# Chunk attention and Fourier mixing on one core: one add moved to VectorE, one weight conversion moved back on ScalarE

## Chip, cores and metric

The kernel runs on one core of a Trainium2 chip. The metric is the device time of one execution in microseconds (us); the time of a kernel is the median of its runs.

## What is computed

q, k, v and the output are float32, the two weights float64. With B = 8 batches, H = 8 heads, S = 576 tokens and D = 64:

```python
# attention in chunks of 64 tokens, each chunk on its own
scores = (q_c @ k_c.T) / sqrt(D)
attn = softmax(scores)
x = (attn @ v_c)                      # bridged to (B, S, 512)
# Fourier mixing and a two-layer network
mixed = real(fft(fft(x, axis=1), axis=2))
u = x + mixed
un = (u - mean(u)) / sqrt(var(u) + 1e-6)
out = u + relu(un @ w_ch1) @ w_ch2    # 512 -> 2048 -> 512
```

## The kernel before

**Tiles.** A tile is 128 tokens by 512 columns. Each batch has two lower tiles (LO, the first four chunks), two upper tiles (HI, the last four, kept mirrored, with a 513th column), and a middle chunk; the middle chunks of two batches share one tile (RE, "rest"). `at[HI, 1, 0]` is the first upper tile of batch 1, the second batch. The upper half of a Fourier transform of real data mirrors the lower half, so `mixed(i)` makes one product `mix` in PSUM for lower tile i and upper tile i together. `both` turns it into `y` on VectorE with two instructions (L850 and L851), and `added` (L857) adds `y` to the rows of each tile in `xall`: the lower and the middle tiles on VectorE, the upper tiles on GpSimd. `means` takes mean and variance of both tiles (VectorE, L705 and L706) and then 1/sqrt(var + eps) of both at once (ScalarE, L709 and L710).

**Groups.** The network runs on groups of four tiles: group g for g = 0 to 7 is batch g, and a ninth group holds the four rest tiles. `normed(g, s)` makes the normalised rows `un` of tile s (for group 1, and for tiles 0 and 1 of group 0, three ScalarE instructions, L996 to L998; otherwise VectorE, L1000). `turned` transposes `un` on TensorE (L399) and copies it out of PSUM to `unT` (L1013). Attention and Fourier mixing of batch b + 1 are woven by hand into the network of group b, step by step. The order on each engine is that in which the program issues the instructions.

**Group 0.** Its network has plain products: w_ch1 at L1219 (with the first weight rows at L944) and w_ch2 at L1260. From group 1 on seven products of halves take the place of eight (L1309 and L1363; the last two groups do the second layer in L1427), with sums and differences of weight blocks that are made once, on GpSimd, while group 0 is still in the network: `keep2` for w_ch2 (L1095) and `keep1` for w_ch1 (L1078). SyncE stores these sums (L1107, L1082, L1114).

**Weight conversion.** The weights arrive as 32 pieces of 128 by 512 float64 values, which the kernel turns into float32 from their bits, as `round_weight(i)` does in a pipeline: the head of piece i and the tail of piece i - 1. The head masks the exponent (VectorE, L372) and the high fraction bits (VectorE, L382), and has three ScalarE instructions: `fraction` (L364, needs L382), `exponent` (L367, needs L372) and `power_` (L370, needs `exponent`). The tail adds the low fraction bits to the fraction (VectorE, L379, needs L364), adds the sign to the power (VectorE, L380, needs L370), and multiplies the two (VectorE, L388). It then frees the piece's landing space and issues the next load (SyncE, L348). A head can be given a list `later`; its three ScalarE instructions are then not issued but put into the list, in the order fraction, exponent, power_. Piece 1 does so in `fourier_early`, with the list `put_off`:

```python
round_weight(1, put_off, "h")     # head only
...
idle[0] = mid
for do in put_off[:2]:            # fraction, exponent
    do()
keep_warm(3)
```

The third, `power_`, follows after the first two pairs of normalised tiles, as `put_off[2]()`. `keep_warm` issues matmuls of no use.

Of the kernel before, what the change touches and what calls it, by code (L numbers as in the profile page):

```python
# [11 lines left out]
ALU = mybir.AluOpType  # L12
# [4 lines left out]
def kernel(  # L17
# [32 lines left out]
    nc = tc.nc  # L50
# [117 lines left out]
    LO, HI, RE = "lo", "hi", "rest"  # L168
# [10 lines left out]
    at = {t: n for n, t in enumerate(tiles)}  # L179
# [17 lines left out]
    def kind(n):  # L197
        return tiles[n][0]
# [140 lines left out]
    def raw(i):  # L339
        return spaces[raws[i]].bitcast(U32).rearrange("p (f r) -> p f r", r=2)  # L340

    def load_weight(i):

        fit = [r for r in free if (i < N_EARLY or r < N_LATE) and (i < N_LAST or r > 1)]
        if i < len(pieces) and fit:
            raws[i] = fit[0]
            free.remove(fit[0])
            nc.sync.dma_start(out=raw(i).rearrange("p f r -> p (f r)"), in_=pieces[i][1].bitcast(U32))  # L348

    def round_weight(i, later=None, parts="ht"):  # L350

        head, tail = "h" in parts and i < len(pieces), "t" in parts and 0 < i <= len(pieces)
        if head:
            w, t = pieces[i][0], raw(i)
            hi, wi = t[:, :, 1], w.bitcast(U32)  # L360
            p = power[i] = three_p.tile([128, 512], U32, tag="o", name="power")

            def fraction(w=w, wi=wi):
                nc.scalar.activation(out=w, in_=wi, func=ACTF.Copy, scale=2.0 ** -20, bias=1.0)  # L364

            def exponent(p=p):
                nc.scalar.activation(out=p, in_=p, func=ACTF.Relu, scale=-1.0, bias=top[:, 0:1])  # L367

            def power_(p=p):
                nc.scalar.activation(out=p, in_=p, func=ACTF.Relu, scale=-8.0, bias=top[:, 1:2])  # L370

            nc.vector.tensor_scalar(p, hi, 0x7FF00000, None, ALU.bitwise_and)  # L372
            if later is None:
                exponent()
                power_()
        if tail:
            w_, t_ = pieces[i - 1][0], raw(i - 1)
            p_ = power.pop(i - 1)
            nc.vector.scalar_tensor_tensor(w_, t_[:, :, 0], 2.0 ** -52, w_, ALU.mult, ALU.add)  # L379
            nc.vector.scalar_tensor_tensor(p_, t_[:, :, 1], 0x80000000, p_, ALU.bitwise_and, ALU.bitwise_or)  # L380
        if head:
            nc.vector.tensor_scalar(wi, hi, 0x000FFFFF, None, ALU.bitwise_and)  # L382
            if later is None:
                fraction()
            else:
                later += [fraction, exponent, power_]
        if tail:
            nc.vector.tensor_tensor(out=w_, in0=w_, in1=p_.bitcast(FP32), op=ALU.mult)  # L388

            r = raws.pop(i - 1)  # L390
            if i - 1 + len(spaces) < N_EARLY or r < N_LATE:
                free.append(r)
            load_weight(max(raws, default=i - 1) + 1)
# [320 lines left out]
    def z_sets(z, pm, i, turn_, first=False):  # L714


        for s in range(2):
            for q_ in range(4):
                k, r = (q_ // 2 + turn_) % 2, q_ % 2
                T, p = 2 * k + s, slice(32 * q_, 32 * q_ + 32)  # L720
                d0_ = T * HQ if i < NM else s * HQ
                nc.tensor.matmul(  # L722
                    out=z[r][k][:, s * NE:(s + 1) * NE], lhsT=pm[i][p, d0_:d0_ + HQ],
                    rhs=tk[p, NM - 1 - i if i < NM else NM, k],
                    start=first and s == 0, stop=False, skip_group_check=True,
                )

    def mid_products(outs, pm, i):
        p, m0 = (slice(0, 128), DM) if i < NM else (slice(CH, 128), 2 * HQ)
        for g, out_ in enumerate(outs):  # L730
            c0, c1 = halves[g % 2]
            nc.tensor.matmul(
                out=out_[:, 0:c1 - c0], lhsT=pm[i][p, m0 + g // 2:m0 + g // 2 + 1], rhs=tk[p, NM - 1 - i if i < NM else NM, 0, c0:c1],
                start=False, stop=i == NM, skip_group_check=True,
            )

    def z_space():


        odd = [ps_t.tile([128, 512], FP32, tag="pt", name="z") for _ in range(2)]  # L740
        even = ps_a.tile([128, 2, 512], FP32, tag="att", name="more_z")
        zs[1:] = even, odd
        return odd, [even[:, k] for k in range(2)]

    def z_odd():
        for k in range(2):
            nc.scalar.copy(zs[0][:, 2 * k:2 * k + 2, 1], zs[2][k][:, 0:2 * NE].rearrange("p (t f) -> p t f", t=2))
# [10 lines left out]
    def z_middle(outs):  # L758
        for g, out_ in enumerate(outs):
            c0, c1 = halves[g % 2]  # L760
            nc.scalar.copy(middle[:, g // 2, c0:c1], out_[:, 0:c1 - c0])
# [33 lines left out]
    def fourier(b):  # L795
        h = b % 2
        zf = one_p.tile([128, 4 * NL + 16], FP32, tag="zf", name="zf")
        zf = zf[:, 0:4 * NL].rearrange("p (t f) -> p t f", t=4)
        zs[0] = one_p.tile([128, 8 * NE], FP32, tag="two", name="zs").rearrange("p (t r f) -> p t r f", t=4, r=2)
        pm = [pms.pop((b, i)) for i in range(NM + 1)]  # L800


        z = z_space()
        for i in range(NM + 1):
            z_sets(z, pm, i, 0, i == 0)
        outs = [z[0][0][32 * g:32 * g + 1, 2 * NE:] for g in range(4)]
        for i in range(NM):
            mid_products(outs, pm, i)
        nc.scalar.copy(middle[:, 0, 0:1], outs[0][:, 0:1])
        yield  # L810
        if b == 1:
            yield True
        mid_products(outs, pm, NM)
        for i in range(NM):
            z_sets(z, pm, i, 1)
        z_middle(outs)
        z_odd()
        if b == 1:
            round_next()
            z_joined()  # L820
        else:
            yield
            z_joined()
        nc.scalar.copy(zs[0][0:1, 2], middle)
        for i in range(NM):
            z_tile(zf, i)
        if h == 0:
            z_rest(h)
        yield

        def mixed(i):
            mix = ps_t.tile([128, 512], FP32, tag="pt", name="mix")
            zt = zr.rearrange("p t h f -> p t (h f)") if i == NM else zf[:, :, 128 * i:128 * (i + 1)]
            for T, (cols, tab) in enumerate((
                (slice(0, HM + 1, 2), ce),
                (slice(1, HM, 2), co),
                (slice(0, DM, 2), cx),
                (slice(HM + 1, DM, 2), so),
            )):
                nc.tensor.matmul(  # L840
                    out=mix[:, cols], lhsT=zt[:, T], rhs=tab,
                    start=(T == 0), stop=(T == 3), skip_group_check=True,
                )
            y = three_p.tile([128, XW], FP32, tag="y", name="y")
            nc.scalar.copy(y[:, 0:HM + 1], mix[:, 0:HM + 1])
            nc.scalar.copy(y[:, DM:DM + 1], mix[:, 0:1])
            return y, mix

        def both(y, mix):
            nc.vector.tensor_tensor(out=y[:, DM - 1:HM:-1], in0=y[:, 1:HM], in1=mix[:, HM + 1:DM], op=ALU.subtract)  # L850
            nc.vector.tensor_tensor(out=y[:, 1:HM], in0=y[:, 1:HM], in1=mix[:, HM + 1:DM], op=ALU.add)  # L851
            return y

        def added(y, n):
            x, w = xt(n), DM + (kind(n) == HI)
            eng = nc.gpsimd if kind(n) == HI else nc.vector
            eng.tensor_tensor(out=x[:, 0:w], in0=y[:, 0:w], in1=x[:, 0:w], op=ALU.add)  # L857

        for i in range(NM + h):
            y = mixed(i)  # L860
            if i == 0 and h == 1:
                z_rest(h)
            y = both(*y)
            ns = [rests[b // 2]] if i == NM else [at[LO, b, i], at[HI, b, i]]
            for n in ns:
                added(y, n)
            means(ns)
            yield

    def fourier_early():  # L870
# [43 lines left out]
        n, m = CH // 2, CH // 4  # L914
# [15 lines left out]
                    start=(T == 0), stop=(T == 2), skip_group_check=True,  # L930
                )
        idle[0] = mid
        for do in put_off[:2]:
            do()
        keep_warm(3)
        yield
        ups = ps_a.tile([128, 2, 512], FP32, tag="att", name="up_a")
# [11 lines left out]
        for i in range(NM):  # L949
# [13 lines left out]
            if i == 0:  # L963
                normed(0, 1)
                turned(0, 0)
                keep_warm(1)
        put_off[2]()
        put_off.clear()
        columns(1)
        normed(0, 2)  # L970
# [490 lines left out]
    with tc.manual_schedule():  # L1461
# [31 lines left out]
        put_off, first_ups = [], []  # L1493

        def round_next(later=None):
            nonlocal n_w
            if n_w <= len(pieces):
                round_weight(n_w, later)
                n_w += 1
# [159 lines left out]
```

## Time and profile before

| | us |
|---|---|
| median of 3 runs | 1060.59 (1060.47 to 1060.66) |
| profiled execution | 1062.15 |
| its span, from the first to the last instruction | 1060.3 |
| TensorE busy | 1043.2 (98%) |
| VectorE busy | 626.4 (59%) |
| GpSimd busy | 431.5 (41%) |
| ScalarE busy | 315.2 (30%) |

The profile is of one execution, and its times count from the start of its span. The granted TensorE clock has a mean of 0.996 of full speed. The busy share is an average over stages that differ: the first 42 us (attention and Fourier mixing of batch 0 before any network can run), the network of group 0 up to about 190 us with all weight conversions beside it, and seven further groups and the rest tiles after it. In the profile PE is TensorE's matmuls, PEld its weight loads, DVE is VectorE, ACT is ScalarE, POOL is GpSimd, SP is SyncE, and L857 is line 857 of the kernel.

### The profile page before, as it was taken

What the parts mean: (1) busy time and instruction counts of PE and PEld (TensorE: products, weight loads), DVE (VectorE), ACT (ScalarE), POOL (GpSimd) and SP (SyncE); (2) the same over time, 40 slices, a digit from 0 to 9 for tenths busy, and PEclk for the clock granted to TensorE, in tenths of its full rate; (3) what the DMA queues carried; (4) which work ended last, traced back from release to release, by engine and by line L of the source; (5) the groups of instructions that cost most, each with busy time, mean ns of one, the idle gap of its engine ahead of it and who ended that gap; (6) DMA issues with size and microseconds to landing.
All of it is one profiled execution on the core that took longest, in us unless ns stands there. A gap on an engine that the chain in (4) does not pass through costs nothing.

```text
span 1060.3 us, 20226 instructions
## 1 busy us (share of the span) xinstructions
PE 1043.2 (98%) x7482; PEld 852.8 (80%) x7482; DVE 626.4 (59%) x1339; ACT 315.2 (30%) x744; POOL 431.5 (41%) x555
## 2 busy tenths in 40 slices
PE   8899998999999999999999999999999999999998
PEld 6655444788888888888888888888888888888887
DVE  3798996874567465664565645735664666543332
ACT  4688573233113311332022312331133102201200
POOL 3401119753425151244134421524252777661272
PEclk8999999999999999999999999999999999999999
DMA  8757666777678447973577358844753759999264
GB/s 163 227 182 221 173 192 227 204 230 240 223 211 236 135 141 222 246 201 110 184 228 225 119 169 233 253 128 154 226 159 100 265 183 352 345 389 321 90 208 149
DMA packets 167088, 219.10 MB, mean 207 GB/s; under 512 B 77228, under 2 KB 111020, under 8 KB 161614
## 3 DMA queue, kind: packets, MB, share of 16 engines
q1 hardware_dynamic: 155978, 211.98, 64.2%
q0 software_dynamic: 9024, 4.91, 2.1%
q8 instruction: 60, 0.98, 0.4%
q10 hardware_dynamic: 1988, 0.92, 0.3%
q14 instruction: 38, 0.31, 0.1%
HBM read 183.61 MB, written 34.08 MB: 205 GB/s over the span
## 4 chain that ended last, share of the span: by engine, by line
PE 86%; DVE 4%; SPq 3%; ACT 3%; DMA 2%; issue 1%; POOL 0%; DVEq 0%; ACTq 0%; POOLq 0%
PE pa L1309 20%; PE pb L1309 15%; PE pb L1363 15%; PE pa L1363 12%; PE dn L1427 8%; PE dn L1260 3%; PE pt L399 3%; PE up L1219 2%; PE z L722 2%; PE xp L501 2%; SPq L265 2%; PE mix L840 2%; DMA xall<-in_moe_w_ch_dram 1%; PE sc L451 1%; PE up_a L1219 0%
## 5 line engine op out<-in xcount | busy, mean ns | idle before, releaser
L1309 PE MATMUL pa<-unT,wa 128*128 128x256 f32 x736 | 175.3, 381 | 0.2 <-DVE xall L1317 0.2
L1309 PEld LDWEIGHTS pa<-unT,wa 128*128 128x128 f32 x736 | 138.1, 190 | 19.6 <-DVE xall L1317 0.6
L1309 PE MATMUL pb<-wa 128*128 128x256 f32 x448 | 106.6, 381 | 0.0
L1309 PEld LDWEIGHTS pb<-wa 128*128 128x128 f32 x448 | 84.3, 190 | 11.5
L1363 PE MATMUL pa<-wb,h 128*128 128x256 f32 x384 | 87.2, 380 | 0.0
L1363 PE MATMUL pb<-wb,h 128*128 128x256 f32 x384 | 86.4, 379 | 0.0
L1193 POOL TENSOR_TENSOR h<-h 128x256 f32<-128x256 f32 x48 | 40.8, 858 | 97.8 <-DVE wb L1191 91.3
L1363 PEld LDWEIGHTS pa<-wb,h 128*128 128x128 f32 x384 | 71.8, 190 | 9.7
L1363 PEld LDWEIGHTS pb<-wb,h 128*128 128x128 f32 x384 | 72.0, 190 | 9.4
L1044 POOL DMA_DIRECT2D out_dram<-wb x28 | 18.8, 674 | 121.1 <-DVE wb L1380 71.9
L1315 DVE TENSOR_TENSOR wa<-pb,wa 128x256 f32<-128x256 f32 x56 | 23.7, 424 | 63.4 <-ACT wa L1314 63.4
L1309 PE MATMUL pb<-unT,wa 128*128 128x256 f32 x256 | 60.6, 379 | 0.1
L1325 ACT ACTIVATE h<-pa 128x256 f32<-128x256 f32 x64 | 24.6, 384 | 115.0 <-PE pa L1309 114.6
L1260 PE MATMUL dn<-wb,h 128*128 128x512 f32 x128 | 57.4, 596 | 0.0
L1314 ACT COPY wa<-pa 128x256 f32<-128x256 f32 x56 | 20.9, 373 | 121.4 <-PE pa L1309 121.4
L1309 PEld LDWEIGHTS pb<-unT,wa 128*128 128x128 f32 x256 | 48.6, 190 | 7.1 <-DVE wa L1315 0.5
L1207 POOL TENSOR_TENSOR h<-h 128x512 f32<-128x512 f32 x34 | 42.6, 1272 | 27.6 <-ACT h L1331 24.1
L1309 PE MATMUL pa<-wa 128*128 128x256 f32 x224 | 53.9, 383 | 0.0
L483 ACT COPY pT<-pt 128x512 f32<-128x512 f32 x36 | 21.0, 583 | 107.2 <-PE pt L399 107.0
L1331 ACT ACTIVATE h<-h 128x512 f32<-128x512 f32 x64 | 39.9, 629 | 39.8 <-DVE h L1330 39.7
L1219 PE MATMUL up<-unT,wa 128*128 128x512 f32 x108 | 49.4, 598 | 0.0
L857 POOL TENSOR_TENSOR xall<-y,xall 128x513 f32<-128x513 f32 x14 | 22.3, 1590 | 61.1 <-DVE y L851 45.0
(312 smaller groups left out, 2138.9 us busy)
## 6 DMA issues: line engine op xcount, KB each, us to landing
wa<-s SPq DMA_DIRECT2D x196, 256.0 KB
wb<-s SPq DMA_DIRECT2D x42, 1024.0 KB
wb<-s SPq DMA_DIRECT2D x32, 512.0 KB
xall<-in_moe_w_ch_dram SPq DMA_DIRECT2D x22, 512.0 KB
q<-in_q_dram SPq DMA_DIRECT2D x96, 112.0 KB
k<-in_k_dram SPq DMA_DIRECT2D x96, 112.0 KB
s<-part SPq DMA_DIRECT2D x32, 256.0 KB
v<-in_v_dram SPq DMA_DIRECT2D x124, 64.0 KB
```

Source lines behind the costliest of these rows:

```text
L399: nc.tensor.transpose(pt[:, j, :], src(j), ident)
L857: eng.tensor_tensor(out=x[:, 0:w], in0=y[:, 0:w], in1=x[:, 0:w], op=ALU.add)
L1193: nc.gpsimd.tensor_tensor(out=h1[:, m, hi], in0=h1[:, m, lo], in1=h1[:, m, hi], op=ALU.subtract)
L1207: eng.tensor_tensor(out=out_, in0=a, in1=b, op=op)
L1219: nc.tensor.matmul(out=up, lhsT=w1[:, kk, m * 128:(m + 1) * 128], rhs=unT[:, kk], start=(kk == 0), stop=(kk == KD - 1), skip_group_check=True,
L1260: nc.tensor.matmul(out=dn, lhsT=h1[:, m, s * 128:(s + 1) * 128], rhs=w2[:, m, :], start=(m == 0), stop=(m == KF - 1),)
L1309: nc.tensor.matmul(out=dst, lhsT=w[:, kk, r], rhs=rhs[o][:, kk], start=(o in (0, 1) and kk == 0), stop=(kk == 1), skip_group_check=True,)
L1315: nc.vector.tensor_tensor(out=b, in0=pbs[r][:, 0], in1=a, op=ALU.add)
L1325: nc.scalar.activation(out=h1[:, m, lo], in_=dst, func=ACTF.Relu)
L1331: nc.scalar.activation(out=h1[:, HF + m], in_=h1[:, HF + m], func=ACTF.Relu)
L1363: nc.tensor.matmul(out=dst, lhsT=lhs[:, m], rhs=w[:, m], start=(o in (0, 2) and m == 0), stop=(m == HF - 1), skip_group_check=True,)
L1427: nc.tensor.matmul(out=dst, lhsT=lhs[:, m], rhs=w[:, m], start=(fresh and not half and m == 0), stop=(m == 3), skip_group_check=True,)
```

## The change

Three edits. In `added`, the upper tile `at[HI, 1, 0]` is added on VectorE; the other upper tiles stay on GpSimd. In `fourier_early`, `exponent` of piece 1 stays at its place, while `fraction` of piece 1 is issued behind `power_`. In `round_weight(2)`, which holds the tail of piece 1, the two tail instructions are issued in the opposite order, so that the one that needs `fraction` comes second.

```diff
@@ round_weight
         if tail:
             w_, t_ = pieces[i - 1][0], raw(i - 1)
             p_ = power.pop(i - 1)
-            nc.vector.scalar_tensor_tensor(w_, t_[:, :, 0], 2.0 ** -52, w_, ALU.mult, ALU.add)
-            nc.vector.scalar_tensor_tensor(p_, t_[:, :, 1], 0x80000000, p_, ALU.bitwise_and, ALU.bitwise_or)
+            for part in (1, 0) if i == 2 else (0, 1):
+                if part == 0:
+                    nc.vector.scalar_tensor_tensor(w_, t_[:, :, 0], 2.0 ** -52, w_, ALU.mult, ALU.add)
+                else:
+                    nc.vector.scalar_tensor_tensor(p_, t_[:, :, 1], 0x80000000, p_, ALU.bitwise_and, ALU.bitwise_or)
@@ added, in fourier
-            eng = nc.gpsimd if kind(n) == HI else nc.vector
+            eng = nc.gpsimd if kind(n) == HI and n != at[HI, 1, 0] else nc.vector
             eng.tensor_tensor(out=x[:, 0:w], in0=y[:, 0:w], in1=x[:, 0:w], op=ALU.add)
@@ fourier_early
         idle[0] = mid
-        for do in put_off[:2]:
-            do()
+        put_off[1]()
         keep_warm(3)
...
         put_off[2]()
+        put_off[0]()
         put_off.clear()
         columns(1)
```

The order of instructions is otherwise unchanged on every engine; the number of instructions is the same. In the changed kernel lines have a number higher by 3 from the first edit on (by 2 between the two edits of `fourier_early`): L857 is L860 there.

## The prediction

> **What bounds the kernel now.** I read the page first, then the table by stage, then what TensorE waited for, then the chain and the timelines at the two places that the diff touches.
>
> ```profile
> PE 1043.2 (98%) x7482; PEld 852.8 (80%) x7482; DVE 626.4 (59%) x1339; ACT 315.2 (30%) x744; POOL 431.5 (41%) x555
> ```
>
> TensorE is busy for 98% of the span, so only what closes one of its few holes can shorten the run. The windows view, with columns for the stretch, PE, PEld, DVE, ACT, POOL busy, clock, DMA share and GB/s, says where they are.
>
> ```profile
> 42.00:54.00 12.00, 10.16 (x66) 8.32 (x66) 10.70 (x25) 10.85 (x38) 0.00 (x0) 1.00 0.57 136
> 160.00:170.00 10.00, 8.42 (x28) 4.17 (x26) 3.62 (x9) 3.22 (x10) 8.72 (x7) 1.00 0.80 249
> 170.00:182.00 12.00, 9.80 (x63) 4.97 (x64) 8.84 (x15) 5.04 (x15) 11.32 (x9) 1.00 0.50 178
> 201.00:1060.00 859.00, 855.01 (x6100) 743.84 (x6099) 466.84 (x1003) 193.14 (x496) 362.35 (x463) 1.00 0.66 209
> ```
>
> The holes lie at 42 to 54 us and at 160 to 182 us. The waits view, asked for TensorE from 205 us on, lists nothing: whatever TensorE gains before 205 us should reach the end unshortened. For 42 to 205 us it lists (total, times, longest):
>
> ```profile
> PE pt L399 <- DVE y L851: 2.6, 2, 2.1
> PE pt L399 <- ACT un L998: 1.6, 2, 1.1
> PE pt L399 <- ACT unT L1013: 1.1, 1, 1.1
> ```
>
> The second line is the hole at 47 us, the other two are at 170 to 182 us. The diff touches both.
>
> **Part 1, the conversion on ScalarE.** The chain of waits around 44 us (start, duration, what):
>
> ```profile
> 44.03 0.10 ACT zr L924
> 44.14 0.52 ACT wa L364
> 44.65 0.61 ACT power L367
> 45.26 0.19 ACT rstd L709
> ```
>
> ScalarE is the path here. `fraction` of weight piece 1 (L364, 0.52) and `exponent` (L367, 0.61) stand ahead of the first rstd; the VectorE result that this rstd needs is complete at 44.40 (L706, 44.22 + 0.18). Taking L364 away starts the rstd 0.52 earlier. The later rstds are not caught by VectorE: their L706 end at 45.98, 47.51 and 49.09, and ScalarE would come to them at 46.33, 48.48 and 49.38. So un moves from 46.13 to 45.61 and TensorE's transposes from 47.00 and 48.68 to 46.48 and 48.16; its idle time there (1.05 and 0.54) covers 0.52.
>
> L364 comes back behind the third late instruction, `power_` (L370), which moves from 50.34 to 49.82. L364 then runs from about 50.45 (0.63 behind L370, as at 53.42 and 54.05) to 51.06. Behind it stands the copy of unT for the third transposes. It starts at 51.69 after 0.64 of idle ScalarE, so at 51.17 after the change: L364 fits with 0.1 to spare, and is costed at nothing. Without that cover, the copy would be late by the overhang, at worst 0.52, and Part 1 would give nothing.
>
> The VectorE instruction that needs L364 is L379 of piece 1. The swap of the two tail instructions puts L380 first, which needs only L370. L380 would run at 50.75 to 51.36, L379 start at 51.36, 0.3 after L364 ends; L388 finishes the piece at 52.97 instead of 53.49. TensorE needs the piece at 53.70 instead of 54.22, so the margin stays 0.73. **Part 1: -0.52.** From there to 160 us the weight pieces' conversions, the attention of the second batch and the loads are released by one another, so they should move together; VectorE's waits for a load (0.67, 1.21 and 0.22 at 140, 144 and 149 us) are on loads issued after its own earlier steps.
>
> **Part 2, the add on VectorE.** The timeline of all engines (start, duration, engine, line, what, idle before and who ended it):
>
> ```profile
> 160.62 0.86 DVE L857 TENSOR_TENSOR xall<-y,xall 128x512 f32<-128x512 f32 x1
> ...
> 160.89 1.71 POOL L1095 TENSOR_TENSOR xall<-wb,xall 128x512 f32<-128x512 f32 x1
> ...
> 161.51 0.69 DVE L705 BATCH_NORM_STATS2 bst<-xall 128x6 f32<-128x512 f32 x1
> ...
> 162.57 1.25 POOL L1095 TENSOR_TENSOR yall<-wb 128x512 f32<-128x512 f32 x1
> ...
> 163.79 1.27 POOL L857 TENSOR_TENSOR xall<-y,xall 128x513 f32<-128x513 f32 x1
> ...
> 165.09 0.69 DVE L705 BATCH_NORM_STATS2 bst<-xall 128x6 f32<-128x512 f32 x1 [2.67 <-POOL xall L857]
> ...
> 166.04 0.30 ACT L709 ACTIVATE rstd<-st,eps 128x2 f32<-128x2 f32 x1 [7.53 <-DVE st L706]
> ```
>
> The upper tile's add stands in GpSimd's queue behind two L1095 (sums of w_ch2) that still have to run when its y is complete, and ends at 165.06; VectorE waits 2.67 for it, then ScalarE's rstd, two normalised row tiles, the copy of the next mix at 169.06, L850, L851 at 169.96, and TensorE's transposes at 170.53, which need the PSUM buffer that L851 frees. All of that is one chain behind the rstd.
>
> After the change the add follows L857 of the lower tile on VectorE, with no wait of its own, and can start at 161.39 (independent neighbours overlap by 0.08). Its price is bounded below by the fastest row of L857 on VectorE, 0.69. It is likely more, since GpSimd is inside an add then. Rows where both engines add from SBUF:
>
> ```profile
> 174.77 1.26 POOL L1078 TENSOR_TENSOR wa<-wa 128x512 f32<-128x512 f32 x1
> 175.01 1.57 DVE L857 TENSOR_TENSOR xall<-y,xall 128x512 f32<-128x512 f32 x1
> ...
> 184.23 1.33 POOL L1095 TENSOR_TENSOR yall<-wb,yall 128x512 f32<-128x512 f32 x1
> ...
> 184.36 1.49 DVE L1033 TENSOR_TENSOR unT<-unT 128x256 f32<-128x256 f32 x1
> ```
>
> At 175.01 VectorE's add ends 0.55 after GpSimd's (176.58 against 176.03): it was held until GpSimd was through. At 184.36 L1033 follows another VectorE add directly, with GpSimd's add waiting since 184.23; GpSimd goes first (ends 185.56) and L1033, alone 0.41, ends at 185.84. The engines alternate. L1095 at 160.89 takes 1.71 because it waited for the lower tile's add; so it goes next, to 162.60, and the upper tile's add ends at 162.60 + 0.55 = 163.15, a price of 1.76. The upper bound is that the four L1095 still to come also go first: 1.23 each (their steps from 165.02 on), 4.92 more. I take 1.76, from the rows nearest in time and operands.
>
> From the add's end to the rstd: L705 (-0.08 + 0.69), L706 (0.04 + 0.18), L705 (-0.09 + 0.69), L706 (0.04 + 0.18), and 0.04 to ScalarE, 1.69 in all. The rstd starts at 164.84 instead of 166.04. TensorE's transposes come at 169.33; it is through with its own work at 168.42, so it still idles 0.9 and gains all of 1.20. The next links (the second upper add, still on GpSimd, which is free by 168.0, before the 169.36 at which that add is now released; its L705; the mix of the middle chunk; TensorE at 175.12 and 181.69) hang on this one and keep their distances. GpSimd's L1095 lose one add ahead of them and gain a wait of 0.55; nothing on TensorE asks for their stores before 205 us. The two y copies on ScalarE get a wait on GpSimd memsets of 120 and 129 us, long done: nothing. **Part 2: -1.20.**
>
> The Trainium skill, GPSIMD Engine Reference, section 4.1 Engine selection, advises VectorE for elementwise adds, GpSimd being about twice as slow with two inputs. The durations alone (0.69 against 1.27) agree with it, and with the bare 0.69 the sum would be the first rival's. The Trainium skill, SBUF — State Buffer, section Who interferes with whom, speaks against that: adds with both inputs in SBUF exclude a GpSimd add for its whole length, and the sum by it is the forecast's.
>
> **The sum.** 0.52 + 1.20 = 1.72. The profiled execution took 1062.15, its span 1060.3 and 1.85 around it; by the sum it would take 1060.43. It lies 1.56 above the median of the runs, 1060.59; the saving is the same there: **1058.9**.
>
> **Rivals.**
> *VectorE keeps the port for two adds in a row.* The add ends at 162.08, the rstd starts at 163.77, 2.27 earlier; with Part 1 2.79, so 1057.8. For it: the lower tile's add is already running. Against: 184.36 and the rows after it.
> *The early saving doesn't last.* Loads for the last weight pieces keep their times, so VectorE waits 0.5 longer at 140 to 149 us, and only 1.20 remains: 1059.4. For it: those three waits on loads. Against: their issues follow VectorE's own steps. If L364 hits the unT copy the result is the same.
> *Slower: GpSimd's queue starves the add.* Without L857 in it, GpSimd has four more L1095 that wait for no other engine. Each that goes ahead of VectorE's add costs 1.23. From the second on, the whole saving of 1.72 is gone: two give 1060.59 - 1.72 + 2.46 = 1061.3, all four 1063.8. Against it: nowhere above does VectorE wait for two.
>
> **How the numbers follow.** Forecast 0.67, first rival 0.15, second 0.10, slower rival 0.08. What a measurement of this kernel can tell from no change is about 0.2%, 2.12 us: faster means under 1058.47, slower over 1062.71. The forecast and the second rival lie inside. Faster is the first rival and 0.08 of the forecast's spread (some 0.3 about 1.72, as the add's hold and the conversions fall): 0.23. Slower is the far end of the starving case: 0.05. Same takes the rest, 0.72. The range, 1057.7 to 1060.4, takes in the first two rivals, and at its upper end a saving of which only 0.2 is left (an add held behind nearly one more L1095); the starving case from two on is left out.
>
> **What would show it.** Right: L364 of piece 1 between L370 and the unT copy, the first un near 45.6, and TensorE's first wait for un 0.5 shorter; a VectorE L857 of 128x513 near 161 us lasting about 1.76, the next rstd 1.2 sooner relative to it, and TensorE's wait on y L851 about 1.2 shorter. Wrong: an upper add of 0.7 (first rival) or of 3 and more (starved); a wait of TensorE for unT at 52 us or for a load later; any new TensorE wait beyond 205 us.

## The result, and the profile after

Median of 17 runs 1058.92 us (1057.18 to 1061.27), beside 1060.56 (1059.23 to 1062.30) for 17 runs of the kernel before; the ratio is 0.9985, 95% interval 0.9978 to 0.9992. The saving is 1.64 us, 0.8 to 2.3 by the interval. The profiled execution took 1058.0, its span 1056.2.

That span is 4.1 shorter than the one before, and half of it is not the change. The windows view of both executions from 10 to 20 us, before first, shows why; the clock is the eighth column.

```profile
10.00:20.00 10.00, 8.38 (x125) 6.63 (x124) 3.74 (x9) 4.20 (x8) 0.00 (x0) 0.66 0.93 182
```

```profile
10.00:20.00 10.00, 8.48 (x198) 6.58 (x202) 5.36 (x13) 6.03 (x13) 0.00 (x0) 1.00 0.93 188
```

TensorE was granted 0.66 of its clock there in one execution and all of it in the other: 125 matmuls against 198 in the same 10 us, long before the first instruction that the diff touches. On ScalarE the same instructions stand 0.20 apart at 12 us and 2.06 apart at 17 us, and still 2.06 at the last `zr` instruction (L924 at 43.93 before, L927 at 41.87 after). Everything below is therefore read by stretches that start there:

- early: from that instruction to the first network products of the third normalised tile (L946)
- middle: to the first `mix` of the second batch's Fourier stage
- late: to the first transposes of group 1 (L402)
- closing: to the first product of `xall` and `wa` (L1312)
- rest: to the end

| us | early | middle | late | closing | rest | sum |
|---|---|---|---|---|---|---|
| before | 8.40 | 102.22 | 15.98 | 30.25 | 859.53 | 1016.39 |
| after | 7.88 | 101.97 | 14.68 | 30.24 | 859.58 | 1014.36 |
| difference | -0.52 | -0.25 | -1.30 | -0.01 | +0.05 | -2.03 |

The middle stretch has nothing of the change in it. Over the runs below and these two it lies between 101.89 and 102.69 with no order that follows the edits: the two kernels with late sums below issue the same work in the same order up to the first `mix`, and have 101.91 and 102.48. So its 0.25 here is scatter. Part of it is a wait of VectorE on a weight load, 1.21 at 143.86 before and 0.99 at 141.06 after.

The windows of the two holes, and TensorE's waits from 42 to 202 us, after:

```profile
42.00:54.00 12.00, 10.68 (x64) 7.97 (x63) 10.54 (x25) 11.23 (x28) 0.00 (x0) 1.00 0.58 131
160.00:170.00 10.00, 9.19 (x31) 4.59 (x29) 5.17 (x13) 4.04 (x14) 8.68 (x7) 1.00 1.01 321
170.00:182.00 12.00, 10.32 (x67) 5.31 (x66) 9.94 (x13) 5.46 (x13) 11.84 (x10) 1.00 0.55 187
```

```profile
PE pt L402 <- DVE y L854: 1.3, 2, 0.8
PE pt L402 <- ACT unT L1016: 1.1, 1, 1.1
PE pt L402 <- ACT un L1001: 1.1, 2, 0.5
...
PE up_a L946 <- ACT unT L1016: 0.2, 1, 0.2
```

The wait for `un` went from 1.6 to 1.1 (the longest from 1.1 to 0.5), the wait for `y` from 2.6 to 1.3 (the longest from 2.1 to 0.8). From 202 us on the waits view lists a single 0.2, so both savings reach the end.

The two places in the timeline, ScalarE first:

```profile
47.76 0.71 ACT L370 ACTIVATE power<-power,top 128x512 uint32<-128x512 uint32 x1
48.38 0.62 ACT L364 ACTIVATE wa<-wa 128x512 f32<-128x512 uint32 x1
49.11 1.08 ACT L1016 COPY unT<-pt 128x512 f32<-128x512 f32 x2
```

`fraction` (L364) runs between `power_` and the copy of unT. Where the next instruction stands ready behind it, that one starts 0.52 later (an experiment below shows it), so 48.90 would be free for the copy and 0.21 is left before it at 49.11.

```profile
157.78 2.54 DVE L860 TENSOR_TENSOR xall<-y,xall 128x512 f32<-128x512 f32 x2
158.05 1.71 POOL L1098 TENSOR_TENSOR xall<-wb,xall 128x512 f32<-128x512 f32 x1
...
159.73 1.72 POOL L1098 TENSOR_TENSOR yall<-wb 128x512 f32<-128x512 f32 x1
...
160.24 0.68 DVE L708 BATCH_NORM_STATS2 bst<-xall 128x6 f32<-128x512 f32 x1
...
161.97 0.29 ACT L712 ACTIVATE rstd<-st,eps 128x2 f32<-128x2 f32 x1 [6.30 <-DVE st L709]
```

The view joins neighbours of one line and prints the shape of the first: the x2 are the lower tile's add and, behind it, the upper tile's, which a window of its own shows:

```profile
158.56 1.75 DVE L860 TENSOR_TENSOR xall<-y,xall 128x513 f32<-128x513 f32 x1
```

Together they take 2.54 and end at 160.32, which is 0.56 after GpSimd's L1098 (158.05 + 1.71 = 159.76). The next L1098 starts at 159.73 and in turn lasts 1.72: the engines alternate. The rstd comes 10.25 behind the first `mix` of the stage (151.72), before 11.49 (166.04 - 154.55): 1.24 sooner. From the start of the lower tile's add it comes after 4.19 (161.97 - 157.78), before after 5.42 (166.04 - 160.62): 1.23 sooner.

### The profile page after: what moved, and what is told of

Read it like the earlier page. It is cut to its first block, busy times and chain, and to the rows that moved or that the text cites. A ratio compares the mean times of both kernels' runs of the same rounds, so it can differ in the third digit from the quotient of the medians.

```text
span 1056.2 us, 20226 instructions
## 1 busy us (share of the span) xinstructions
PE 1041.6 (99%) x7482; PEld 851.5 (81%) x7482; DVE 627.6 (59%) x1340; ACT 314.9 (30%) x744; POOL 431.0 (41%) x554
## 4 chain that ended last, share of the span: by engine, by line
PE 80%; DVE 6%; DMA 4%; SPq 3%; ACT 3%; POOL 2%; issue 2%; DVEq 0%; ACTq 0%; POOLq 0%
PE pa L1312 21%; PE pb L1312 15%; PE pb L1366 14%; PE pa L1366 11%; PE dn L1430 9%; PE pt L402 2%; DMA xall<-in_moe_w_ch_dram 2%; PE mix L843 2%; SPq L265 2%; PE xp L504 2%; PE z L725 1%; PE sc L454 1%; PE up L1222 1%; DVE power L383 1%; POOL part L1159 1%
## 5 line engine op out<-in xcount | busy, mean ns | idle before, releaser
L1312 PE MATMUL pa<-unT,wa 128*128 128x256 f32 x736 | 175.3, 381 | 0.2 <-DVE xall L1320 0.2
L1312 PEld LDWEIGHTS pa<-unT,wa 128*128 128x128 f32 x736 | 138.1, 190 | 19.6 <-DVE xall L1320 0.6
L1312 PE MATMUL pb<-wa 128*128 128x256 f32 x448 | 106.6, 381 | 0.0
L1312 PEld LDWEIGHTS pb<-wa 128*128 128x128 f32 x448 | 84.3, 190 | 11.5
L1318 DVE TENSOR_TENSOR wa<-pb,wa 128x256 f32<-128x256 f32 x56 | 23.7, 424 | 63.5 <-ACT wa L1317 63.5
L1312 PE MATMUL pb<-unT,wa 128*128 128x256 f32 x256 | 60.6, 379 | 0.2 <-DVE wa L1318 0.2
L1312 PEld LDWEIGHTS pb<-unT,wa 128*128 128x128 f32 x256 | 48.6, 190 | 7.1 <-DVE wa L1318 0.6
L1312 PE MATMUL pa<-wa 128*128 128x256 f32 x224 | 53.9, 383 | 0.0
L1312 PEld LDWEIGHTS pa<-wa 128*128 128x128 f32 x224 | 41.8, 190 | 6.2
```

The lines of the kernel that those rows point to most:

```text
L1312: nc.tensor.matmul(out=dst, lhsT=w[:, kk, r], rhs=rhs[o][:, kk], start=(o in (0, 1) and kk == 0), stop=(kk == 1), skip_group_check=True,)
L1318: nc.vector.tensor_tensor(out=b, in0=pbs[r][:, 0], in1=a, op=ALU.add)
```

## Experiments

All are edits of the changed kernel, in the numbering of that kernel. Where a kernel has one run, its time is given and the conclusion rests on the stretches. The early stretch repeats to 0.01 among kernels with the same conversion. The late one is 14.68 to 14.69 in the changed kernel and in the three edits of it that leave this stretch alone. But its start, the first `mix`, can lie some 0.25 differently against VectorE's work. The stretch from the lower tile's add to the rstd is free of that.

**Each part alone.**

```diff
# conversion only
-            eng = nc.gpsimd if kind(n) == HI and n != at[HI, 1, 0] else nc.vector
+            eng = nc.gpsimd if kind(n) == HI else nc.vector
```

> The change without its add: the first upper tile is added on GpSimd again; the move of the fraction and the swap of the two tail instructions stay. Read by stretches inside one profile, since spans differ by their starts: early = from the last copy of zr on ScalarE to TensorE's third set of first-row matmuls (before 52.33 - 43.93 = 8.40, after 7.88), late = from TensorE's first mix of the second batch to the first transposes of group 1 (before 15.98, after 14.68), closing = from there to the L1309 matmuls of before's 200.78 (30.25 in both). My theory, two savings independent of each other: early 7.88, late 15.98, closing 30.25. Rival, the early saving only shifts a wait that batch 1's chain meets again: early 7.88, late or middle longer by up to 0.5.

```diff
# add only: the old tail order, and in fourier_early
-        put_off[1]()
+        for do in put_off[:2]:
+            do()
...
         put_off[2]()
-        put_off[0]()
```

> The change without its conversion part: fraction and exponent at their old place, tail instructions in the old order; the add on VectorE stays. My theory: early 8.40 as before, late 14.68 with a VectorE add of 1.76 to 1.8 for the upper tile. Rival, the late saving needs the earlier start (another relation of loads and conversions at 150 us): late between 14.7 and 16.0.

| us | early | middle | late | closing | rest | one run |
|---|---|---|---|---|---|---|
| conversion only | 7.88 | 101.90 | 15.73 | 30.25 | 860.14 | 1059.45 |
| add only | 8.39 | 101.89 | 14.46 | 30.24 | 859.59 | 1057.69 |

The parts separate cleanly. The early stretch is short exactly where the conversion is moved, by 0.51 to 0.52; the late one where the add is moved, by 1.05 (15.73 to 14.68) to 1.52 (15.98 to 14.46). That spread is the start of the stretch: the lower tile's add begins 6.06 to 6.07 behind the first `mix` before and after the change, and 5.82 and 5.84 in these two. From the lower tile's add to the rstd it is 5.42 before and with the conversion only, and 4.18 to 4.19 after and with the add only: the moved add is worth 1.23 to 1.24 with or without the conversion. The second rival, an early saving that is lost between 140 and 149 us, would show as a middle stretch 0.5 longer in the conversion-only kernel than in the add-only one; it is 0.01 longer. As this stretch scatters by up to 0.8, two traces alone would not settle it, but seven of the nine traces with the moved conversion have 101.9 to 102.2, like the two without (101.89 and 102.22). The conversion-only kernel's rest is 0.6 longer than before and after the change; 0.5 of it arises between 877 and 903 us, 700 us behind the edits, and the cause is open.

**The swap of the two tail instructions.**

```diff
-            for part in (1, 0) if i == 2 else (0, 1):
+            for part in (0, 1):
```

> The changed kernel with the two tail instructions of piece 1 in their old order. My theory: the first of them waits some 0.3 for the fraction, the product of piece 1 ends 0.3 later (of 0.73 that it has), nothing else moves: early 7.88 and the first full matmuls on piece 1 without a wait. Rival, the swap carries the early saving: TensorE waits for piece 1, or the later pieces run late and the stretch from the early anchor to the first mix grows from 101.97 by 0.3.

Early 7.88, late 14.69, 1058.72 in one run: the same without the swap, and TensorE has no wait for piece 1. The product of piece 1 ends 0.37 before TensorE needs it (51.81 against 52.18), with the swap 0.73 before: what the piece has in hand covers either order. The swap is worth nothing.

**How thick the cover of L364 is.** One more ScalarE copy of 128x512 behind L364, into a tile that is idle then.

```diff
         put_off[0]()
+        nc.scalar.copy(tk..., early_tk...)   # 128 x 512
```

> The changed kernel with one more ScalarE copy of 128x512 (of tables, into a buffer that is written again later) right behind the moved fraction, ahead of the unT copies. My theory: the fraction lies in a hole of 0.64 with 0.1 to spare, so the extra copy (about 0.46 a step) pushes the unT copy and TensorE's third first-row matmuls back by 0.35: early 8.2, four fifths of the early saving gone... if its step is 0.57, early 8.34. Rival, the hole is wider than it looks, since the copy waits for TensorE: early stays 7.88.

Early 8.16, 0.28 longer. ScalarE's timeline:

```profile
47.28 0.71 ACT L370 ACTIVATE power<-power,top 128x512 uint32<-128x512 uint32 x1
47.90 0.62 ACT L364 ACTIVATE wa<-wa 128x512 f32<-128x512 uint32 x1
48.42 0.60 ACT L971 COPY tk<-wb 128x512 f32<-128x512 f32 x1
48.93 1.06 ACT L1017 COPY unT<-pt 128x512 f32<-128x512 f32 x2
```

```profile
PE pt L402 <- ACT un L1002: 1.1, 2, 0.5
PE up_a L946 <- ACT unT L1017: 0.5, 1, 0.5
```

The copy of unT now follows without idle time (48.42 to 48.93 is the step of 0.51), and TensorE's wait for it grows from 0.2 to 0.5. So 0.2 to 0.3 of ScalarE time was free there: the cover existed, and it was thin. With this one instruction more Part 1 gives back 0.28 of its 0.52.

**Is it GpSimd that holds the add?** The sums of w_ch2 (L1098) that stand beside the adds are put off to a later step; nothing else is touched.

```diff
-                if n_w > len(pieces):
+                if n_w > len(pieces) and t > 25:
                     for _ in range(3):
```

> The changed kernel with GpSimd's sums of w_ch2 started one step later, behind the second upper tile's add, so that GpSimd is idle while VectorE adds the first pair of tiles. My theory, the price of 1.76 is the hold of a port by GpSimd's add: the upper tile's add takes 0.69, the rstd of the first pair comes 1.2 sooner (1.8 with two conversion steps that are also held now), late falls by TensorE's remaining wait of 0.81 from 14.68 to about 13.9, and some 0.5 to 1.0 more in the closing stretch. Rival, the price is that of a second add with 513 columns right behind another: it stays near 1.76, late 14.1 or more. Second rival, the delayed sums collide later: late 13.9, closing longer by as much.

```profile
156.69 1.30 DVE L860 TENSOR_TENSOR xall<-y,xall 128x512 f32<-128x512 f32 x2
...
157.91 0.68 DVE L708 BATCH_NORM_STATS2 bst<-xall 128x6 f32<-128x512 f32 x1
...
159.63 0.29 ACT L712 ACTIVATE rstd<-st,eps 128x2 f32<-128x2 f32 x1 [4.47 <-DVE st L709]
```

The upper tile's add alone, behind the lower one:

```profile
157.30 0.69 DVE L860 TENSOR_TENSOR xall<-y,xall 128x513 f32<-128x513 f32 x1
```

With GpSimd silent the same two adds take 1.30 instead of 2.54, and the rstd follows the first of them by 2.94 instead of 4.19. The 1.24 between the two sums of adds is the hold, shown by itself: 1.06 on the upper tile's add (1.75 to 0.69) and 0.17 on the lower one (0.86 to 0.69). The rival, a price of the 513 columns, is refuted by the 0.69. The late stretch falls to 13.60, 1.08 below the change, the closing one to 29.75, and TensorE has no wait for `y` left; there is nothing more to be had from the add.

The run as a whole took 1059.58, no better than before the change, since the rest grew by 3.2 to 862.81. The timelines of VectorE and SyncE beyond 195 us say where:

```profile
205.83 1.10 DVE L421 STREAM_TRANSPOSE qT<-q 128x512 f32<-128x512 f32 x1 [4.89 <-DMA q<-in_q_dram]
206.77 0.73 DVE L1318 TENSOR_TENSOR xall<-pb,xall 128x256 f32<-128x256 f32 x2
```

```profile
189.85 2.78 SPq L1110 DMA_DIRECT2D s<-yall  x4
192.68 0.52 SPq L1085 DMA_DIRECT2D s<-wa  x1
193.29 6.01 SPq L275 DMA_DIRECT2D v<-in_v_dram  x4
199.36 0.97 SPq L1085 DMA_DIRECT2D s<-wb  x1
200.42 1.85 SPq L252 DMA_DIRECT2D q<-in_q_dram  x4
```

SyncE issues in order, and the stores of the sums (L1110) stand ahead of the loads for the next attention. Later sums make later stores, and the load of v starts at 193.29 instead of 188.32, that of q at 200.42 instead of 195.90. VectorE waits 4.89 for q, its L1318 stands behind that wait, and TensorE waits 1.8 for L1318 and then 0.5 for the transposed k (L421), whose load is late too. With what follows each wait, 2.7 of the 3.2 are lost up to there. The sums may be off TensorE's path; the queue of their stores is not.

**The other upper tile on VectorE too.**

```diff
-            eng = nc.gpsimd if kind(n) == HI and n != at[HI, 1, 0] else nc.vector
+            eng = nc.gpsimd if kind(n) == HI and n not in (at[HI, 1, 0], at[HI, 1, 1]) else nc.vector
```

> The changed kernel with the second batch's other upper tile on VectorE as well. Port theory: GpSimd, which waits for nothing then, runs its next sums through VectorE's two adds; the lower add ends 0.7 later than alone, the upper one is held behind one more sum, and the second rstd comes 1.3 later (after: 169.09): late 14.68, closing 31.5, the whole 1.3 slower. Rival, VectorE's adds are simply shorter than GpSimd's (0.69 against 1.71): the second rstd within 0.2, closing 30.2.

The near half of the expectation held, the far half didn't. VectorE and GpSimd of this kernel:

```profile
166.36 2.40 DVE L860 TENSOR_TENSOR xall<-y,xall 128x512 f32<-128x512 f32 x2
...
182.10 0.41 DVE L1034 TENSOR_TENSOR xall<-unT 128x256 f32<-128x256 f32 x1
```

```profile
168.17 1.72 POOL L1081 TENSOR_TENSOR wa<-wa 128x512 f32<-128x512 f32 x1
...
180.45 1.44 POOL L1098 TENSOR_TENSOR yall<-wb,yall 128x512 f32<-128x512 f32 x1
```

In the changed kernel GpSimd was no obstacle to this add: it was idle when the add came, and ran it at once.

```profile
166.40 1.71 POOL L860 TENSOR_TENSOR xall<-y,xall 128x513 f32<-128x513 f32 x1 [1.16 <-DMA s<-wb]
```

On VectorE the add is held by the next sum, the second rstd comes 1.25 later (170.41 - 151.79 = 18.62 behind the first `mix`, against 169.09 - 151.72 = 17.37), and TensorE's second transposes 1.24 later relative to the first (5.84 against 4.60). But the closing stretch is 0.42 shorter, not longer. TensorE's wait for unT before the fourth transposes falls from 1.1 to 0.3, which returns 0.9 of the delay. And GpSimd's sums, one add the fewer, are through at 181.89 instead of 184.25, and from then on VectorE's L1034 to L1036 run unheld, 0.41 to 0.42 each; in the changed kernel at the same place:

```profile
181.64 1.48 DVE L1034 TENSOR_TENSOR xall<-unT 128x256 f32<-128x256 f32 x1
183.16 1.37 DVE L1035 TENSOR_TENSOR xall<-unT,xall 128x256 f32<-128x256 f32 x1
...
185.73 0.67 DVE L1276 TENSOR_TENSOR o<-dn,xall 128x512 f32<-128x512 f32 x1
```

L1276 starts at 184.15 instead of 185.73, and TensorE's waits of 0.3 and 0.2 behind it (for `h` and `xall`, up to 196.65 in the changed kernel) are gone. One run took 1057.61; with a difference of 0.4 in the closing stretch and scatter of that size in the middle one, better or equal to the change is not settled.

**What is late next.** After the change the path from the rstd runs through two normalised tiles on ScalarE, then the copy of the next `mix`, then `y`, then TensorE. The copy doesn't need the tiles. Here it goes ahead of them.

```diff
             y = mixed(i)
+            if (b, i) == (1, 1):
+                normed(1, 0)
+                normed(1, 1)
...
-                if m == (9, 9, 11, 11)[j]:
+                if m == (-1, -1, 11, 11)[j]:
```

> The changed kernel with ScalarE's copy of the second mix ahead of the first two normalised tiles of group 1 instead of behind them. If TensorE's wait on L851 is only this order on ScalarE (rstd, two un, then the copy): the copy comes 2.4 sooner, TensorE's first transposes wait for nothing (late 13.9), the second rstd 1.15 sooner as GpSimd's queue then bounds the upper add: closing 29.9, the whole 1.15 faster than after. Rival, un becomes the wait in its place: late 14.4 or more.

```profile
161.62 0.20 ACT L713 ACTIVATE rstd<-rstd 128x2 f32<-128x2 f32 x1
161.74 0.36 ACT L848 COPY y<-mix 128x257 f32<-128x257 f32 x1
161.99 0.16 ACT L849 COPY y<-mix 128x1 f32<-128x1 f32 x1
162.04 0.21 ACT L1002 ACTIVATE shift<-st 128x1 f32<-128x1 f32 x1
```

The copy (L848, L849) starts 0.12 behind the second rstd instruction, and the wait for `y` is gone from TensorE's list. Late 13.61, closing 29.83, rest 859.66, one run 1056.23.

**Both together.**

```diff
# as above, and
-                if n_w > len(pieces):
+                if n_w > len(pieces) and t > 25:
```

> The changed kernel with both e5 and e7: GpSimd's sums one step later, ScalarE's copy of the second mix first. My theory: neither port nor queue holds the chain, TensorE's waits of 0.81, 0.53 and most of 1.14 go: late 13.9, closing 28.7, 2.4 faster than after, 1056.5 us, a ratio to before of 0.996. Rival, GpSimd's delayed sums hold VectorE's adds at 180 to 200 us and give part of it back: closing 29.5 or more.

Closing 28.31 is the shortest of all here, and late 13.71 is close to the 13.60 and 13.61 of the two edits alone; the rest is 864.15, 4.6 longer. The median of 12 runs is 1059.72 beside 1060.35 (ratio 0.9996, 0.9982 to 1.0009): by the interval no saving is left, and what was won is lost behind the closing stretch, where neither the forecast nor its rival had put a loss. TensorE's waits from 202 us on:

```profile
PE pb L1315 <- POOL wa L1084: 2.8, 1, 2.8
```

It is the place at 206.7 us that the previous experiment with late sums had lost 1.8 at (there the view names VectorE's L1318). In this kernel the load of q is late again, VectorE waits 5.9 for it up to 205.23, and L1321, the same instruction as L1318 above, stands behind. That the view names GpSimd's sum is a coincidence of ends (206.65): in the kernel of that experiment the same product started at 207.32, before the same sum had even begun (207.67). The sooner TensorE arrives, the longer it waits. The wait is 2.8 of the 4.6; another 1.7 goes with the granted clock, which is half right behind it in this execution:

```profile
207.20:210.60 3.40, 3.40 (x31) 2.31 (x34) 2.06 (x5) 0.00 (x0) 0.67 (x1) 0.50 0.60 189
```

In the kernel of that experiment, after its wait of 1.8 at this place, the same window has a clock of 1.00.

**The reordered copy, timed.**

> The changed kernel with the normalised rows of group 1's first two tiles issued on ScalarE behind the copy of the second lower tile's mix instead of ahead of it, and with the time of it measured in rounds beside the kernel before. The look at it showed the stretch up to the first transposes of group 1 at 13.61 us (14.68 with the change alone) and the closing stretch at 29.83 (30.24). Theory: rows and closing together are worth 1.07 + 0.41 = 1.5 us on top of the change's own saving of about 1.7, since nothing behind 200 us takes it back (859.66 there against 859.58). So the median should lie 3.1 to 3.2 us below the kernel before, near 1057.4, a ratio near 0.9970. Rival: the 1.5 us of the single look came from the scatter of loads and of the start; then the ratio is the change's own, 0.9985, about 1058.9.

Median 1056.70 of 8 runs beside 1059.67 of 12 for the kernel before: ratio 0.9972, 0.9962 to 0.9983, a saving of 3.0. The stretches of its profile are near those of the single run (late 13.71, closing 30.06, rest 859.61); a wait of 0.4 for `y` is left before the second transposes. This is faster than the kernel before. That it is faster than the changed kernel too is shown by the traces alone, 1.2 to 1.5 in late and closing together: the two intervals against the kernel before (0.9978 to 0.9992 and this one) still overlap.

## Why the prediction was right

**The forecast's mechanism held in both parts, and the total was near:** 1.72 predicted, 1.64 between the medians. The parts measured in the traces add up to 0.52 + 1.23 = 1.75. That the time of 1058.9 met the median of 1058.92 so closely is luck: the interval leaves the saving anywhere from 0.8 to 2.3.

*Part 1, predicted -0.52:* -0.52 in the trace, and the same alone. The cover was predicted as 0.1, from the end of L364's row, and by that measure it is 0.11 (49.00 to 49.11); by the step to a next instruction that stands ready it is 0.2 to 0.3. The margin of 0.73 came out as predicted. It is also why the swap, argued for as the step that keeps L379 in time, turned out to be worth nothing: without it 0.37 is left.

*Part 2, predicted -1.20:* the rstd came 1.23 to 1.24 sooner relative to its stage, the wait for `y` fell by 1.3. The step on which it hung, a held add that ends 0.55 behind GpSimd's, was right to 0.01: two adds predicted at 0.77 + 1.76 = 2.53 measured 2.54. What was argued from other places before is shown by the kernel in which GpSimd is silent: 1.30. The Trainium skill, SBUF — State Buffer, Who interferes with whom, says that a VectorE instruction with two inputs in SBUF contends with a GpSimd instruction that reads SBUF, and calls the shared port pair an exclusive lock. The rows at 157.78 to 159.73 agree with that, and they add what the sum needed, whose turn comes next when both have an add waiting: that of the engine that has been held longer, which costs VectorE 1.24 over its two adds.

*What it missed.* The hold was seen as a matter of this one add. VectorE pays it in other places too where GpSimd sums beside it (L1034 to L1036: up to 1.48 against 0.41), and it works both ways: the second upper tile loses 1.25 at its own add, gets 0.9 back out of TensorE's wait for unT, and gets more back later, where the sums end sooner. The prediction's remark that GpSimd loses one add and gains a wait stopped short of that, though for the tile of this change nothing came of it. The prediction also took the way from the rstd to TensorE as one chain; its link from the normalised tiles to the copy of the next `mix` is only the order on ScalarE, as the reordered copy shows.

*The rivals.* VectorE keeping the port: refuted by the 2.54. Its price for the rstd was near: it has the rstd 3.15 behind the start of the lower tile's add (163.77 - 160.62), and with GpSimd silent it is 2.94. But its sum passed all of the 2.27 on to TensorE, which before the change idled only 2.11 there (168.42 to 170.53). The early saving lost: refuted by the middle stretches. The starved add: refuted by the 2.54 too, which has room for one L1098 and no second.

*The likeliest time* was set against a profiled execution 1.56 above the median, with its saving carried over unchanged. That held, and a reason was seen only after: beside the changed kernel's execution, that one had lost about 2 us before 20 us, where its clock was low and the change has no part.

## What to carry to other kernels

Where an add of this shape with both inputs in SBUF is moved from GpSimd to VectorE while GpSimd goes on adding, cost it as the end of GpSimd's current or waiting add plus 0.55, not at its own 0.69. It pays when GpSimd's queue stood longer in the way than that (1.24 here); where GpSimd was idle, the next step came 1.25 later. When a wait gets shorter, compare every gain with the idle time that TensorE has left, and look along the chain for a step that needs none of it: here one copy that stood behind two normalised tiles was worth about as much as the whole change. Before work off the path is put off, see which loads stand behind its stores in the same queue.

## What the runs showed that was not expected

The clock granted to TensorE between 10 and 20 us differs between executions of nearly the same program, 0.66 in the trace before and 1.00 in the ten others, and the trace with the lower clock is 1.9 us further behind at 17 us than at 12 us, more than the change is worth. In one execution, of the kernel with both edits, the clock was also 0.50 from 207.2 to 210.6 us, right behind a wait of TensorE of 2.8. The runs of the kernel before spread over 3.1 us (1059.23 to 1062.30), so single runs can't rank these kernels; stretches of a trace with their own starting point can.
